# A fused attention and SwiGLU kernel: one hand-paced order replaced by a build-time planner, with batch 0 in two halves

## Chip, cores and metric

The kernel runs on one core of a Trainium2 chip. The metric is the device time of one execution in microseconds (us); times of several executions are given as a median.

The core's engines work side by side, each through its own queue in order: PE (matrix products, with PEld its weight loads), DVE (elementwise), ACT (functions and copies), POOL (here mostly the issue of loads) and SP (the issue of transposing DMAs and of output stores). They wait for each other by semaphores. Products land in PSUM, eight banks of 512 fp32 columns on 128 partitions; ACT and DVE must empty a bank before it is used again.

## The reference

Attention with squared ReLU in place of softmax, for 8 batches and 12 heads, 448 tokens, head size 64; then an RMS norm and a gated FFN on the 3584 tokens by 768 features.

```python
def _attn_ref(q, k, v):
    scale = 1.0 / np.sqrt(q.shape[-1])
    scores = scale * np.matmul(q, k.transpose(0, 1, 3, 2))
    attn = np.maximum(scores, 0.0) ** 2 / S
    return np.matmul(attn, v)

def _moe_ref(x, w_gate, w_val, w_out, rms_g):
    rms = np.sqrt(np.mean(x * x, axis=-1, keepdims=True) + 1e-06)
    xn = x / rms * rms_g
    g = xn @ w_gate
    silu = g * (1.0 / (1.0 + np.exp(-g)))
    val = xn @ w_val
    return silu * val @ w_out
```

Inputs and output are fp32 in memory; the kernel loads them as bf16 and accumulates in fp32. The hidden width is 1536.

## The kernel before

**Products by halves of the array.** The head size is 64, so PE's array is used as two row halves of 64 rows: two products, one on each half, run at the same time. A pair of them is called a step here. The class `Stream` (L306) pairs the two halves of the FFN's products: a `Group` (L357) is one output tile; first its lower half runs as the leading one of the pair while the group before it runs its upper half, then it follows. `emit` (L375) writes one half product and, when a group changes halves, a wait on PE for its own last product.

**Attention of one batch** (`attention`, L281) goes over six pairs of heads `j`. For batches 0 and 1 q and k are turned by PE (`transposes`, L169, copied by DVE, L182); later ones by transposing DMAs on SP (`transpose_dma`, L100). `scores` (L208) computes 128 keys by 448 queries for two heads into a pair of PSUM banks (psS), three times per `j`; the last 64 keys of two `j` share one tile (`rest_scores`, L221). `rectify` (L197) empties each: relu to bf16 on ACT (L202) or DVE (L200) by the fixed table `relu_on`, then a square in place on DVE (L205), for three tiles of batch 0 on POOL. `attend` (L238) multiplies by v for two `j` as 64-by-64 products on the four quarters of the array (psAV); ACT scales into xT (L276) and DVE squares xT into x2 (L278).

**Norm.** `norm_sums` (L402; `norm`, L408, for batch 0) multiplies the six tiles of x2 by a matrix of ones: six steps into psSS. `norm_scale` (L418) takes the square root on ACT (L420), loads the SiLU table, takes the reciprocal on DVE (L424) and scales xT to xn in six instructions (L427).

**FFN.** `ffn` (L503): 12 gate and 12 value groups of six steps of 448 columns (psP), emptied by `silu` on ACT (L451) and by `hidden` on DVE (L456) into hT. Then output tiles of 128 tokens, in three pieces of 256 columns (`OW`, L474), 12 steps each (psO): three tiles after an even batch, four after an odd one, as two batches share 7 tiles. `store` (L486) copies on ACT (L490) and, after the third piece, issues the output from SP (L498).

**Order.** Loads of batch 0, the gate and value weights in eight slices, then batch 0's attention and norm run alone; `keep_busy` (L137) writes products of zeros on PE into psB, 16 at the start, one after each `scores` and 24 during the norm. Loads of batch 1 and w_out stand in POOL's order after that. From then the loop at L523 lays the attention of batch b+1 as `side` units between the FFN steps of batch b, evenly by a cost that counts columns. The sum for the norm goes to the front of the stream after the last attend.

PSUM: two pairs of banks for scores and attends (`ps_s`) and four single banks for all else (`ps_m`).

Of the kernel before, what the change touches and what calls it, by code (L numbers as in the profile page):

```python
# [9 lines left out]
I32 = mybir.dt.int32  # L10
# [4 lines left out]
NCH = 4  # L15
U = 7
UH = 4


@with_exitstack  # L20
def kernel(
# [22 lines left out]
    NT = 2 * S // P  # L44

# [6 lines left out]
    apool = ctx.enter_context(tc.tile_pool(name="attn", bufs=12))  # L52
    xpool = ctx.enter_context(tc.tile_pool(name="xT", bufs=1))
    npool = ctx.enter_context(tc.tile_pool(name="norm", bufs=2))
    hpool = ctx.enter_context(tc.tile_pool(name="hT", bufs=2))
    spool = ctx.enter_context(tc.tile_pool(name="sig", bufs=3))
    opool = ctx.enter_context(tc.tile_pool(name="ostage", bufs=3))
    ps_s = ctx.enter_context(tc.tile_pool(name="ps_s", bufs=2, space=bass.MemoryType.PSUM))
    ps_m = ctx.enter_context(tc.tile_pool(name="ps_m", bufs=4, space=bass.MemoryType.PSUM))

    ld = {}
    qkT = {}
    src_of = {"q": q, "k": k, "v": v}
    PE_T = 2

    def load(nm, b, h0=0, h1=H):
# [7 lines left out]
        t = ld[nm, b]  # L76
        src = src_of[nm][b, h0:h1]
        if nm == "q":
            parts = [(slice(0, PC), PC, 0, NCH)]
        else:  # L80
            parts = [(slice(0, D), D, 0, UH), (slice(D, P), D, UH if nm == "k" else UH - 1, U)]
        for prt, n, u0, u1 in parts:
            if runs:
                nc.gpsimd.dma_start(  # L84
                    out=t[prt, h0:h1, : (u1 - u0) * D],
                    in_=src.rearrange("h (p u) d -> p h (u d)", p=n)[:, :, u0 * D : u1 * D],
                )
            else:
                to = t[prt].rearrange("p u (h d) -> p u h d", d=D)
                rows = src.rearrange("h (p u) d -> p u h d", p=n)  # L90
                step = u1 - u0 if nm == "q" else 1
                for u in range(u0, u1, step):
                    nc.gpsimd.dma_start(  # L93
                        out=to[:, u - u0 : u - u0 + step, h0:h1, :], in_=rows[:, u : u + step]
                    )

    def new_qkT(b):
        qkT[b] = qtpool.tile([P, HP, 2, S], BF16, name="qkT", tag="qkT")

    def transpose_dma(b):  # L100
        new_qkT(b)
        for c in range(UH):
            n = P if c < UH - 1 else D
            nc.sync.dma_start_transpose(
                out=qkT[b][:, :, 0, c * P : c * P + n], in_=ld["k", b][:n, c, :]
            )
        for c in range(NCH):
            nc.sync.dma_start_transpose(
                out=qkT[b][:, :, 1, c * PC : (c + 1) * PC], in_=ld["q", b][:, c, :]
            )  # L110
# [5 lines left out]
    FS = F // NSL  # L116

    def load_w(which, s):
        dst, src = {"g": (wg_sb, moe_w_gate), "v": (wv_sb, moe_w_val)}[which]
        nc.gpsimd.dma_start(  # L120
            out=dst[:, :, s * FS : (s + 1) * FS],
            in_=src.rearrange("(kt p) f -> p kt f", p=P)[:, :, s * FS : (s + 1) * FS],
        )

    def load_wo(s, n):
        w = FT // n
        nc.gpsimd.dma_start(
            out=wo_sb[:, s * w : (s + 1) * w, :],
            in_=moe_w_out.rearrange("(fk p) m -> p fk m", p=P)[:, s * w : (s + 1) * w, :],
        )  # L130
# [5 lines left out]

    def keep_busy(n):  # L137
        ps = ps_m.tile([P, S], FP32, name="psB", tag="mm")
        for _ in range(n):
            nc.tensor.matmul(out=ps[:], lhsT=ones_bf[:], rhs=busy_bf[:], start=True, stop=True)  # L140

    load("q", 0, 0, 2)
    load("k", 0, 0, 2)
    ident = const.tile([P, P], BF16, name="ident", tag="ident")
    masks.make_identity(nc, ident[:])
# [3 lines left out]

    def act_table(func):  # L150
        nc.scalar.activation(out=scrap[:], in_=eps_col[:], func=func)

    act_table(ACT.Sqrt)
    g_sb = wpool.tile([P, KT], FP32, name="g_sb", tag="rmsg")
    nc.sync.dma_start(out=g_sb[:], in_=moe_rms_g.rearrange("(kt p) -> p kt", p=P))
    load("q", 0, 2, 6)
    load("k", 0, 2, 6)
    load("v", 0, 0, 6)
    load("q", 0, 6, 12)
    load("k", 0, 6, 12)  # L160
    load("v", 0, 6, 12)
    for s in range(NSL):
        load_w("g", s)
        load_w("v", s)

    behind = mybir.DependencyInfo(mybir.DependencyClass.Sync, mybir.DependencyReason.DATA)
    xTs = {}

    def transposes(b, j):  # L169
        if j == 0:  # L170
            new_qkT(b)
        psT = ps_m.tile([P, 2, S], BF16, name="psT", tag="mm")
        flat = psT[:].rearrange("p t s -> p (t s)")
        for nm, n, w, at in (("k", P, UH, 0), ("q", PC, NCH, S)):
            for c in range(w):
                for hh in range(2):
                    nc.tensor.transpose(  # L177
                        out=flat[hh * D : (hh + 1) * D, at + c * n : at + (c + 1) * n],
                        in_=ld[nm, b][:, 2 * j + hh, c * D : (c + 1) * D],
                        identity=ident[:n, :n],  # L180
                    )
        nc.vector.tensor_copy(out=qkT[b][:, j, :, :], in_=psT[:])  # L182

    rsq = {}
    pending = []

    def relu_on(b, j, c):
        return "dve" if c == UH - 1 or (b and j % 2 and c == 2) else "act"

    def square_on(b, j, c):  # L190
        return "pool" if b == 0 and j >= 3 and c == 1 else "dve"

    def flush():
        while pending:
            pending.pop(0)()

    def rectify(b, j, c, psS):  # L197
        r = apool.tile([P, 2, S], BF16, name="r", tag="r")
        if relu_on(b, j, c) == "dve":
            nc.vector.tensor_relu(out=r[:], in_=psS[:, :, :S])  # L200
        else:
            nc.scalar.activation(out=r[:], in_=psS[:, :, :S], func=ACT.Relu)  # L202
        eng = nc.gpsimd if square_on(b, j, c) == "pool" else nc.vector
        flush()
        pending.append(lambda: eng.tensor_tensor(out=r[:], in0=r[:], in1=r[:], op=ALU.mult))  # L205
        rsq[b, j, c] = r

    def scores(b, j, c):  # L208
        psS = ps_s.tile([P, 2, 512], FP32, name="psS", tag="psS")
        for hh in range(2):  # L210
            prt = slice(hh * D, (hh + 1) * D)
            nc.tensor.matmul(  # L212
                out=psS[:, hh, :S],
                lhsT=qkT[b][prt, j, 0, c * P : (c + 1) * P],
                rhs=qkT[b][prt, j, 1, :],
                start=True,
                stop=True,
            )
        rectify(b, j, c, psS)

    def rest_scores(b, j):  # L221

        psS = ps_s.tile([P, 2, 512], FP32, name="psS", tag="psS")
        for hh in range(2):
            prt = slice(hh * D, (hh + 1) * D)
            for jj in range(2):
                nc.tensor.matmul(  # L227
                    out=psS[jj * D : (jj + 1) * D, hh, :S],
                    lhsT=qkT[b][prt, j + jj, 0, (UH - 1) * P : (UH - 1) * P + D],
                    rhs=qkT[b][prt, j + jj, 1, :],  # L230
                    start=True,
                    stop=True,
                )
        return psS

    x2s = {}

    def attend(b, j, then=None):  # L238
        psAV = ps_s.tile([P, 2, 512], FP32, name="psAV", tag="psS")
        v = ld["v", b]  # L240
        rest = rsq[b, j, UH - 1]
        low, high = slice(0, D), slice(D, P)
        pairs = {
            low: [[(rsq[b, j + jj, i], i) for i in range(UH - 1)] for jj in range(2)],
            high: [[(rsq[b, j + jj, i], i + 1) for i in range(UH - 1)] for jj in range(2)],
        }
        pairs[low][0].append((rest, UH - 1))
        pairs[high][1].append((rest, 0))
        last = {}

        def run(first):
            for step in range(UH - (not first)):
                for prt, jj in ((low, 0), (high, 1)) if first else ((low, 1), (high, 0)):
                    r, u = pairs[prt][jj][step]
                    for hh in range(2):
                        if not first and step == 0:
                            tc.add_manual_dep(nc.tensor.nop().ins, last[jj, hh].name, behind)
                        mm = nc.tensor.matmul(  # L258
                            out=psAV[hh * D : (hh + 1) * D, jj, :S],
                            lhsT=v[prt, 2 * (j + jj) + hh, u * D : (u + 1) * D],  # L260
                            rhs=r[prt, hh, :],
                            start=(first and step == 0),
                            stop=(not first and step == UH - 2),
                        )
                        last[jj, hh] = mm.ins

        run(True)
        psR = rest_scores(*then) if then else None
        run(False)
        if j == 0:  # L270
            xTs[b] = xpool.tile([P, KT, S], BF16, name="xT", tag="xT")
            x2s[b] = npool.tile([P, KT, S], BF16, name="x2", tag="x2", bufs=1)
        xT = xTs[b][:, j : j + 2, :]
        if then:
            rectify(*then, UH - 1, psR)
        nc.scalar.mul(out=xT, in_=psAV[:, :, :S], mul=inv_attn)  # L276
        pending.append(
# [302 lines left out]
```

## Time and profile before

| | |
|---|---|
| runs | 467.36, 470.43, 467.46 us; median 467.46 |
| span of the profiled execution, first to last instruction | 466.5 us (its own time is not listed apart) |
| mean granted clock of PE | 0.982 of full |
| HBM read, written | 48.76 MB, 11.01 MB |
| last matmul starts | 461.2 us |

The costliest groups, by line (us busy and mean ns of one):

| group | count | busy | mean |
|---|---|---|---|
| L380 psP, gate and value products | 2268 recorded | 456.8 | 349 |
| L380 psO, 256 columns | 2016 | 139.6 | 271 |
| L202 relu on ACT, 128x896 from PSUM | 123 | 111.1 | 918 |
| L205 square on DVE, 128x896 bf16 | 165 | 100.9 | 628 |
| L456 hidden on DVE, 128x448 | 96 | 59.5 | 620 |
| L451 silu on ACT, 128x448 | 96 | 51.9 | 542 |
| L200 relu on DVE, 128x896 from PSUM | 45 | 49.1 | 1090 |
| L490 output copy on ACT, 128x256 | 84 | 30.5 | 372 |
| L427 xn on DVE, 128x448 | 48 | 29.3 | 680 |
| L424 reciprocal on DVE, 128x448 | 8 | 23.6 | 2953 |
| L276 xT on ACT, 128x896 | 24 | 22.0 | 917 |
| L140 psB, products of zeros | 58 | 17.6 | 418 |

A product's duration includes its way through the array, and two to four run at once, so the busy time of single products is no cost; the distance between starts is. Some matmul records are missing (2268 of 2304 psP products are there). Start times in the views are in us from the first instruction; "<-" names what a group writes and reads.

### The profile page before, as it was taken

The numbers are of one execution on the slowest core, as the hardware profiler recorded it, in microseconds if no ns is written. First come the engines' busy times: TensorE is split into PE (matmuls) and PEld (weight loads), VectorE is DVE, ScalarE is ACT, GpSimd is POOL, SyncE is SP. The second block draws the span as 40 slices with busy tenths as digits, with TensorE's granted clock in tenths as the row PEclk, the third lists the DMA queues.
The fourth block names the chain that finished last, engine by engine and source line by source line (L and its number), as shares of the span: only waits on it lengthen the run. The fifth ranks groups of instructions, "written<-read, shape, count | busy, mean of one in ns | idle before, by whom it ended". The sixth has DMA issues, their size and how long they took to land.

```text
span 466.5 us, 12798 instructions
## 1 busy us (share of the span) xinstructions
PE 453.6 (97%) x5722; PEld 292.8 (63%) x5722; DVE 274.0 (59%) x403; ACT 234.9 (50%) x360; POOL 80.6 (17%) x97
## 2 busy tenths in 40 slices
PE   6989999999999999999999999999999999999995
PEld 3434655676666766676666766676667766676674
DVE  1676378866663867576566657576656677332200
ACT  1682246665645655375445755465535764532221
POOL 8438211571007000340007000100000000000000
PEclk8698999999999999999999999999999999999998
DMA  9999999799907970299209960438002200020013
GB/s 106 194 204 199 206 173 162 80 204 165 127 3 107 214 124 2 23 200 146 44 1 124 211 109 1 58 82 135 20 1 54 85 2 1 2 84 20 1 42 95
DMA packets 130758, 44.47 MB, mean 95 GB/s; under 512 B 102928, under 2 KB 127120, under 8 KB 130704
## 3 DMA queue, kind: packets, MB, share of 16 engines
q0 software_dynamic: 91648, 24.39, 54.1%
q1 hardware_dynamic: 39056, 19.28, 20.5%
q8 instruction: 44, 0.72, 0.6%
q14 instruction: 10, 0.08, 0.0%
HBM read 48.76 MB, written 11.01 MB: 128 GB/s over the span
## 4 chain that ended last, share of the span: by engine, by line
PE 91%; DVE 3%; ACT 2%; DMA 1%; POOL 1%; issue 1%; POOLq 0%
PE psP L380 47%; PE psO L380 23%; PE psAV L258 8%; PE psS L212 6%; PE psSS L380 2%; ACT r L202 2%; PE psB L140 1%; PE psT L177 1%; PE psS L227 1%; DMA kb<-in_k_dram 1%; DVE xn L427 1%; PE psP L441 1%; DVE r L200 1%; DVE r L205 1%; DVE rstd L424 1%
## 5 line engine op out<-in xcount | busy, mean ns | idle before, releaser
L380 PE MATMUL psP<-xn,wv_sb 64*128 64x448 bf16 x1140 | 229.0, 349 | 0.0
L380 PE MATMUL psP<-xn,wg_sb 64*128 64x448 bf16 x1128 | 227.8, 349 | 0.1
L380 PE MATMUL psO<-wo_sb,hT 64*128 64x256 bf16 x2016 | 139.6, 271 | 0.0
L202 ACT ACTIVATE r<-psS 128x896 bf16<-128x896 f32 x123 | 111.1, 918 | 47.5 <-PE psS L212 46.8
L380 PEld LDWEIGHTS <-wv_sb 64*128 64x128 bf16 x1140 | 96.1, 94 | 41.5 <-issue 4.3
L380 PEld LDWEIGHTS <-hT 64*128 64x128 bf16 x2016 | 101.1, 94 | 33.0 <-issue 2.9
L380 PEld LDWEIGHTS <-wg_sb 64*128 64x128 bf16 x1128 | 94.3, 94 | 35.6 <-issue 1.3
L205 DVE TENSOR_TENSOR r<-r 128x896 bf16<-128x896 bf16 x165 | 100.9, 628 | 16.3 <-ACT r L202 15.6
L456 DVE TENSOR_TENSOR hT<-sil,psP 128x448 bf16<-128x448 bf16 x96 | 59.5, 620 | 79.7 <-PE psP L380 52.4
L451 ACT ACTIVATE sil<-psP 128x448 bf16<-128x448 f32 x96 | 51.9, 542 | 74.7 <-PE psP L380 68.8
L200 DVE TENSOR_SCALAR r<-psS 128x896 bf16<-128x896 f32 x45 | 49.1, 1090 | 31.7 <-PE psS L227 24.2
L212 PE MATMUL psS<-qkT 64*128 64x448 bf16 x288 | 59.3, 358 | 1.9 <-DVE r L200 1.2
L490 ACT COPY ost<-psO 128x256 f32<-128x256 f32 x84 | 30.5, 372 | 43.5 <-PE psO L380 39.6
L276 ACT ACTIVATE xT<-psAV 128x896 bf16<-128x896 f32 x24 | 22.0, 917 | 54.4 <-PE psAV L258 50.1
L258 PE MATMUL psAV<-r,vb 64*64 64x448 bf16 x672 | 43.9, 361 | 1.8 <-POOL r L205 1.2
L84 POOL DMA_DIRECT2D vb<-in_v_dram x18 | 13.2, 750 | 167.7 <-PE psO L380 122.3
L424 DVE RECIPROCAL rstd<-rstd 128x448 f32<-128x448 f32 x8 | 23.6, 2953 | 26.0 <-ACT rstd L420 26.0
L93 POOL DMA_DIRECT2D kb<-in_k_dram x42 | 33.0, 1008 | 18.7 <-DMA wo_sb<-in_moe_w_out_dram 9.6
L258 PEld LDWEIGHTS <-vb 64*64 64x64 bf16 x672 | 17.3, 106 | 22.3 <-issue 10.3
L427 DVE SCALAR_TENSOR_TENSOR xn<-xT,g_sb,rstd 128x448 bf16<-128x448 bf16 x48 | 29.3, 680 | 0.3
L212 PEld LDWEIGHTS <-qkT 64*128 64x128 bf16 x288 | 19.8, 94 | 11.4 <-issue 6.2
L140 PE MATMUL psB<-busy_bf,ones_bf 128*128 128x448 bf16 x58 | 17.6, 418 | 1.3 <-DVE busy_bf L135 1.3
(38 smaller groups left out, 161.7 us busy)
## 6 DMA issues: line engine op xcount, KB each, us to landing
vb<-in_v_dram POOLq DMA_DIRECT2D x14, 384.0 KB, 7.2
qb<-in_q_dram POOLq DMA_DIRECT2D x7, 672.0 KB, 12.9
kb<-in_k_dram POOLq DMA_DIRECT2D x43, 96.0 KB, 12.7
out_dram<-ost SPq DMA_DIRECT2D x8, 336.0 KB, 4.1
wg_sb<-in_moe_w_gate_dram POOLq DMA_DIRECT2D x4, 576.0 KB, 16.5
wv_sb<-in_moe_w_val_dram POOLq DMA_DIRECT2D x4, 576.0 KB, 18.1
wo_sb<-in_moe_w_out_dram POOLq DMA_DIRECT2D x2, 1152.0 KB, 21.4
out_dram<-ost SPq DMA_DIRECT2D x8, 288.0 KB, 4.4
```

Of the source, the lines that this page charges most:

```text
L93: nc.gpsimd.dma_start(out=to[:, u - u0 : u - u0 + step, h0:h1, :], in_=rows[:, u : u + step])
L200: nc.vector.tensor_relu(out=r[:], in_=psS[:, :, :S])
L202: nc.scalar.activation(out=r[:], in_=psS[:, :, :S], func=ACT.Relu)
L205: pending.append(lambda: eng.tensor_tensor(out=r[:], in0=r[:], in1=r[:], op=ALU.mult))
L212: nc.tensor.matmul(out=psS[:, hh, :S], lhsT=qkT[b][prt, j, 0, c * P : (c + 1) * P], rhs=qkT[b][prt, j, 1, :], start=True, stop=True,)
L258: mm = nc.tensor.matmul(out=psAV[hh * D : (hh + 1) * D, jj, :S], lhsT=v[prt, 2 * (j + jj) + hh, u * D : (u + 1) * D], rhs=r[prt, hh, :], s ...
L380: mm = nc.tensor.matmul(out=self.ps[:, : self.w], lhsT=self.lhsT(i)[prt], rhs=self.rhs(i)[prt], start=(half == 0 and i == 0), stop=(half = ...
L424: nc.vector.reciprocal(out=rstd[:], in_=rstd[:])
L427: nc.vector.scalar_tensor_tensor(out=xn[:, kt, :], in0=xTs[b][:, kt, :], scalar=g_sb[:, kt : kt + 1], in1=rstd[:], op0=ALU.mult, op1=ALU.mult,
L451: nc.scalar.activation(out=s[:], in_=psG[:], func=ACT.Silu)
L456: nc.vector.tensor_tensor(out=hTs[b // 2][:, fb, o : o + S], in0=sil[b, fb][:], in1=psV[:], op=ALU.mult)
L490: nc.scalar.copy(out=ost[:, o : o + w], in_=ps[:, :w])
```

## The change

The whole order is now made when the kernel is built, by a `Planner`: each instruction group is an `Op` with assumed durations on the engines it may run on, what it depends on, a rank, and the PSUM banks and ring buffers it needs. The planner walks a simulated time: at each point it takes the engine that can start something first, and there the ready operation of lowest rank. Relu and output copies go to ACT or DVE, whichever the plan has free first. The operations are written out in that order.

- Batch 0 is attended in two halves of 224 queries (`halves`, `HS`), each with its own norm and its own 24 gate and value groups of 224 columns; from batch 1 on the width is 448.
- The norm: ACT takes a logarithm and then exp(-0.5 x), both in one table set (`LN_EXP`), in place of root and reciprocal. DVE adds the squares of the three pairs in fp32 (`square`, `close`), so the sum over features is one product with ones, except in batch 0's first half.
- Output pieces are 384 columns wide, two to a tile (`OW`); copies go to ACT or DVE.
- Groups of 448 columns are emitted as four 64-by-64 quarter products per step (`quarters`), scores beside them too.
- xT, xn and rstd have two buffers; squares never run on POOL; hT has one buffer in place of two; 14 relu buffers in place of 12.
- All loads of batches 0 and 1 and the weights are issued at the start, v of batch 0 after q and k; products of zeros (`fill`) stand where the plan finds PE idle.

```diff
+    def choose(self, e):
+        cands = self.candidates(e)
+        step = None
+        if e == "PE" and self.stream is not None:
+            step = self.stream.earliest()
...
+        for r, rank, n, op, s in cands:
+            if r <= t + 1e-9:
+                if op.due is not None:
+                    rank = -1 if op.due() else 1
+                key = (rank, n)
+                if best is None or key < best[0]:
+                    best = (key, op, s)
...
+    pairs = [psum.tile([P, 2, 512], FP32, name=f"psS{i}", tag=f"psS{i}") for i in range(4)]
+    wide = [Space(pairs[i], (2 * i, 2 * i + 1)) for i in range(4)]
+    single = [Space(pairs[i // 2][:, i % 2, :], (i,)) for i in range(4, 8)]
...
+    def blocks():
+        return ((0, D), (D, P)) if state["quarters"] else ((0, P),)
...
+        rl = add(Op({"ACT": 0.14 + n * 0.833e-3, "DVE": 0.13 + n * 1.042e-3}, relu,
+                    [t] + r_ring.before, rank=2, lean={"DVE": 0.9}))
+        on = {"DVE": 0.06 + n * 0.53e-3}
+        sq = add(Op(on, square, [rl], rank=3))
...
+        def square(op):
+            x = xTs[b][:, j : j + 2, lo : lo + w]
+            acc = accs[b, lo][0][:, :, :w]
+            dst = x2[:, :, :w] if j else acc
+            nc.vector.tensor_tensor(out=dst, in0=x, in1=x, op=ALU.mult)
+            if j:
+                nc.vector.tensor_tensor(out=acc, in0=acc, in1=dst, op=ALU.add)
+
+        def close(op):
+            acc, total, _ = accs[b, lo]
+            nc.vector.tensor_tensor(
+                out=total[:, :w], in0=acc[:, 0, :w], in1=acc[:, 1, :w], op=ALU.add
+            )
...
+            act_set(LN_EXP)
+            nc.scalar.activation(
+                out=rstd[:, :w], in_=g.ps[:, :w], func=ACT.Ln, scale=1.0 / float(DM),
+                bias=eps_col[:],
+            )
+            nc.scalar.activation(out=rstd[:, :w], in_=rstd[:, :w], func=ACT.Exp, scale=-0.5)
...
+            state["quarters"] = any(g.quarters for _, g in pair)
+            for m in blocks():
+                for half, g in pair:
+                    g.emit(half, *m)
...
+        op = add(Op({"ACT": lambda: 0.14 + w * 0.833e-3 + switch(SILU)}, fn, [g.end], rank=0,
+                    ring=sil_ring))
...
-    OW = DM // 3
+    OW = DM // 2
...
+    attention_half(0)
+    stream.add([norm_sums(0, 0, HS)])
     for b in range(B):
+        groups = ffn(b)
         if b == 0:
+            stream.add(groups[:24])
+            plan.run(lambda: (0, 0) in summed)
+            attention_half(HS)
+            attention_full(1)
+            stream.add(groups[24:])
+            sums = [norm_sums(0, HS, HS), norm_sums(1, 0, S)]
```

## The prediction

> **What bounds the kernel now.** I read the engine totals first, then the chain of waits in order of time, then the PE timeline inside one stage, then the DMA issues. The totals, first list of the page (busy us, share, instructions):
>
> ```profile
> PE 453.6 (97%) x5722; PEld 292.8 (63%) x5722; DVE 274.0 (59%) x403; ACT 234.9 (50%) x360; POOL 80.6 (17%) x97
> ```
>
> PE is almost always busy, DVE and ACT little over half. The ends of matmuls are modelled, so 97% does not say that all of it is needed; the chain does (start us, us, what). The opening:
>
> ```profile
> 5.15 4.30 DMA kb<-in_k_dram
> ...
> 34.87 1.40 DVE r L205
> 36.27 0.04 issue
> 36.31 2.27 PE psAV L258 x18
> ...
> 40.81 4.65 PE psB L140 x24
> 45.45 3.53 PE psP L441 x36
> ```
>
> Until 45.4 no FFN product runs: batch 0's attention goes from engine to engine, and psB, which computes nothing, covers its norm. Then the chain is PE nearly to the end, with one more hole before batch 1's FFN:
>
> ```profile
> 95.49 0.64 ACT rstd L420
> 96.13 0.02 issue
> 96.15 2.96 DVE rstd L424
> 99.12 0.02 issue
> 99.14 3.68 DVE xn L427 x6
> ```
>
> PE works through that on output pieces; batch 1's FFN really starts at 102.4. Later stretches are pure PE, here around batch 4:
>
> ```profile
> 289.31 1.32 PE psP L380 x14
> ...
> 297.77 0.11 PE psO L380
> 297.88 0.08 PE psP L380
> ...
> 308.92 0.90 PE psO L380 x16
> ```
>
> Fourteen half products are seven steps (both row halves at once), so a 448-column step is 0.189 us; sixteen psO are eight steps of 256 columns, 0.1125 each. Where both widths meet, the chain alternates: the narrow half idles. The PE timeline at an attend (start, us, then the group):
>
> ```profile
> 179.64 0.35 PE L380 MATMUL psP<-xn,wv_sb 64*128 64x448 bf16 x1
> 179.92 0.95 PE L258 MATMUL psAV<-r,vb 64*64 64x448 bf16 x16
> 180.93 0.79 PE L258 MATMUL psAV<-r,vb 64*64 64x448 bf16 x12
> 181.66 0.36 PE L380 MATMUL psP<-xn,wg_sb 64*128 64x448 bf16 x1
> ```
>
> From the psP step at 179.64 to the next at 181.66 lie 2.02 us. Eight quarter steps (32 instructions with four rest scores) and one psP step make 9 x 0.189 = 1.70; about 0.3 goes at the changes of shape and the in-order wait inside. I take 0.2 an attend as theirs.
>
> **Part by part.** The sum is made against the span, 466.5; the median of the runs is 467.46, 1.0 above. The profiled execution's own time is not listed apart, so I put 1.0 around the span.
>
> *Steady part, 102.4 to PE's end at 461.2.* It holds six batches' attentions, seven projections and 25 output tiles.
>
> - Sum for the norm: six psSS steps become one, since DVE adds the squares first. 5 x 0.189 x 6 batches = 5.7. Twelve steps that pair 448 with 256 columns go as well: the narrow half loses 0.189 - 0.1125 = 0.077 in each, half of the array: 12 x 0.077 / 2 x 6 = 2.8.
> - Pieces of 384: interpolating the two step rows (0.0004 us per column) gives 0.164, an estimate. A tile costs 24 x 0.164 = 3.93 for 36 x 0.1125 = 4.05; 25 tiles save 3.0. Bounds: nothing gained, or 5. The meeting of widths is cheaper, 0.189 - 0.164 = 0.025 for 0.077: 12 steps a batch x 0.052 / 2 x 7 = 2.2.
> - Quarter products: projections of full width and scores are emitted as four 64-by-64 products, the shape of attends, so the change of shape goes: 18 attends x 0.2 = 3.6. PE's instructions in these steps double. The attend shows four loads and four products per 0.189 us step (16 in 0.88, chain), so I cost the doubling at nothing, though its longest run is 32 products.
>
> Sum 17.3.
>
> *Engines beside it.* Between 263.2 and 368.5 (two batches, 105.3 us) DVE is busy 68.4 and ACT 59.0. A batch loses the reciprocal (2.95) and three bf16 squares (0.62 each) and gets five fp32 squares or adds of 896 plus a half one. No fp32 tensor product is in the trace; the nearest rows bound it by 0.63 (L205, bf16) and 1.09 (L200, fp32 read from PSUM). I take 1.0, as it reads or writes fp32: 5.5 - 4.8 = +0.7 us a batch, hidden under 18 us of idle DVE; uncovered it would cost 0.7 x 7 = 5. ACT gains one more pass of 0.63 a batch, with one table set for log and power, so still two loads of 1.28. Both have cover. Two-tile norm buffers let the next norm run ahead.
>
> The Trainium skill, "VectorE: DVE Perf Modes", section "The perf-mode tier table", puts fp32 tensor_tensor at the slowest rate; an estimate from its formula, (896+151)/0.96 ns, is 1.09 us, at my upper row, and would make the batch +1.2.
>
> *Batches 0 and 1.* Transfers do not get shorter. The weight slices land in a row, the last of eight 24.0 us after its issue at 18.1:
>
> ```profile
> wv_sb<-in_moe_w_val_dram POOLq DMA_DIRECT2D x1, 576.0 KB, 24.0
> ```
>
> That is 42.1; the first value slice landed at 24.3 (11.3 + 13.0), so a slice takes 3.0 us. Half of batch 0: evictions and squares are half of before, the last q and k land at 15.7 (8.45 + 7.2); chain by rows: last scores, 0.9 eviction, 0.6 square, products, 0.5 out, squares, two passes, xn, about 9 us: FFN from about 25 in place of 45.4. But it is paced by slices to 42, and batch 1's q and k (1344 KB at 192 KB/us) end at 49, so the twenty us do not all count. What counts is when batch 1's FFN can start. From 47 its attention needs, by rows: 21 evictions (20 us), 21 squares (13), copies (3.7), xT (2.8), squares for the norm (5.6), with batch 0's second-half silu and products (8.4) and output copies (2.9): 56 us over ACT and DVE, 28 each, 31 at 90% use, then norm 4. That is 82; with 4 for unevenness, **86**, instead of 102.4: 16.4 gained. PE has 54 us of products for 25 to 86, so it is not the limit here, even if the 224-column steps of batch 0 (0.100 by the same interpolation, against a 94 ns load that must fit) take 0.11: 288 x 0.01 = 3 us, inside the 7 spare. Fill products stand only where the plan sees PE idle. Bounds: 80 if nothing waits, 98 if late transfers (w_out, 61.9 before) hold the output pieces.
>
> Loads of batch 1 come in ten issues for five on POOL, which now holds no squares (1.70 each on POOL, now 0.63 on DVE); nothing but loads is queued there. On SP, transposes and output stores share the queue as before.
>
> *What the plan costs.* Each engine's order is fixed from assumed durations: square 0.535 (row 0.628), relu on ACT 0.886 (0.918), silu 0.513 (0.542). Per batch 21 x 0.093 + 21 x 0.032 + 12 x 0.03 = 3.0 us too little. In-order PE waits where a product was put just behind an eviction, with the whole FFN stream queued after it. If all lateness reached PE: 7 x 3 = 21. As idle time of a third on both engines takes most, I take 4.
>
> Sum: 466.5 - 17.3 - 16.4 + 4 = 436.8, time **438**. Own range 428 to 449 (batch 1's start 80 to 96, plan 0 to 10). The tail from PE's end, 5.3 us, stays.
>
> **Rivals.**
>
> 1. *The plan drifts* (0.13): the 21 us reach PE instead of 4: 455. For it: only two pairs of PSUM banks for scores and attends, so PE waits at once when a relu is late. Against: the present order, paced without any model, lets PE run unbroken.
> 2. *The head gives nothing* (0.06): batch 1's FFN starts at 98, as transfers and ACT/DVE set it: 450.
> 3. *Quarters are issue-bound*, the slower case (0.08). The densest long row is psO: four instructions per 0.1092 to 0.1125 us, 27 to 28 ns each. If 27.3 were the floor, eight take 0.218, not 0.189: 7 x 144 projections and about 200 others, 1,210 steps x 0.029 = 35: 473. It decides above 0.217 a step. Against: the attend's 23.6 ns an instruction, and psO fits its columns without a floor.
> 4. *Gains cancel* (0.04): half of each of these, 463 to 472.
>
> The Trainium skill, "TensorEngine Tiling (Array Packing)", section "Tiling Modes", says that a change of mode drains the array, which agrees in sign with the 0.3 above; its section "Restrictions and Gotchas" speaks against the change: column tiling gives up fast weight load. The row shows 105 ns for a 64*64 load and 94 for 64*128. If the two loads of a row half came one after the other, 210 ns would exceed 189 and 1,210 steps would cost 25 us, giving 463; the attend's rows speak against that.
>
> **How the numbers follow.** Forecast 0.69, rivals 0.13, 0.06, 0.08, 0.04. The range 426 to 457 takes in the forecast and the first two and leaves out rivals 3 and 4 and a little below. About 1% is what can be told from no change. Faster by over 1% (below 462.8): 0.87; within: 0.05; slower: 0.08.
>
> **What would show it.** Right: first psP of batch 0 near 25, of batch 1 near 86; step 0.189 in quarters and 0.16 in pieces; one sum step; no gap at attends. Wrong: quarter steps over 0.2; PE waiting on relu, square or xn in every batch; DVE over 80% busy; PE waiting on w_out.

## The result, and the profile after

The changed kernel takes 597.04 us (median, 595.80 to 597.47), against 467.63 us of the kernel before in the same session: a ratio of 1.276, 95% interval 1.272 to 1.280. The forecast was 438, with a range of 426 to 457. The profiled execution has a span of 594.9 us, 128 more than before.

The totals of the kernel after, first list of its page (busy us, share of the span, instructions):

```profile
PE 493.9 (83%) x7789; PEld 311.9 (52%) x7789; DVE 250.4 (42%) x411; ACT 273.0 (46%) x388; POOL 78.5 (13%) x99
```

DVE has less to do than before and ACT 38 us more, both under half of the span. No engine became the bound; PE's share fell from 97% to 83%. The chain that ended last, by engine and by line:

```profile
PE 76%; DVE 10%; ACT 10%; issue 3%; DVEq 0%; ACTq 0%
PE psS L738 61%; DVE hT L802 8%; PE psS L537 7%; ACT sil L788 5%; PE psS L424 4%; ACT ost L859 2%; PE psS L965 2%; PE psS L368 1%; ACT r L406 1%; DVE x L574 1%; ACT xT L564 1%; PE psS L460 1%; PE psS L442 1%; DVE acc L576 0%; DVE qkT L378 0%
```

Before, PE had nearly all of it:

```profile
PE 91%; DVE 3%; ACT 2%; DMA 1%; POOL 1%; issue 1%; POOLq 0%
```

Now 23% of the chain, 137 us, is not PE, and most of that lies on the three lines that empty the FFN's banks: hT, sil and ost, 15% of the span together. The waits say who waits for them (engine and line, waited for: us in all, times, longest us):

```profile
PE psS L738 <- DVE hT L802: 51.0, 76, 0.8
...
PE psS L738 <- ACT sil L788: 21.6, 40, 0.6
...
PE psS L738 <- ACT ost L859: 10.8, 20, 0.6
```

PE waited for none of these before. One place shows the form of it: the last batch's FFN, where no attention runs beside it. The timeline of the kernel after (start us, us, what; in brackets the idle time before and what ended it):

```profile
530.17 0.54 ACT L788 ACTIVATE sil<-psS 128x448 bf16<-128x448 f32 x1 [3.53 <-PE psS L738]
530.77 0.35 PE L738 MATMUL psS<-xn,wg_sb 64*64 64x448 bf16 x1 [0.63 <-ACT sil L788]
...
532.20 0.62 DVE L802 TENSOR_TENSOR hT<-sil,psS 128x448 bf16<-128x448 bf16 x1 [3.45 <-PE psS L738]
...
532.88 0.35 PE L738 MATMUL psS<-xn,wv_sb 64*64 64x448 bf16 x1 [0.78 <-DVE hT L802]
```

ACT had been idle for 3.53 us and DVE for 3.45, so neither is late. PE finishes a group, stands while that group's bank is read, and only then begins the next one, although four banks are there and two groups are in work at a time. A group takes 2.0 to 2.1 us; six steps of 0.189 are 1.13. The windows view of the whole stretch (us, then busy us of PE, PEld, DVE, ACT, POOL; clock, DMA share, GB/s):

```profile
515.80:568.40 52.60, 35.24 (x633) 21.95 (x633) 6.84 (x11) 7.49 (x14) 0.00 (x0) 1.00 0.06 17
```

### The profile page after: what moved, and what is told of

It is laid out like the page before. It is cut to its first block, busy times and chain, and to the rows that moved or that the text cites. A ratio compares the mean times of both kernels' runs of the same rounds, so it can differ in the third digit from the quotient of the medians.

```text
span 594.9 us, 16977 instructions
## 1 busy us (share of the span) xinstructions
PE 493.9 (83%) x7789; PEld 311.9 (52%) x7789; DVE 250.4 (42%) x411; ACT 273.0 (46%) x388; POOL 78.5 (13%) x99
## 4 chain that ended last, share of the span: by engine, by line
PE 76%; DVE 10%; ACT 10%; issue 3%; DVEq 0%; ACTq 0%
PE psS L738 61%; DVE hT L802 8%; PE psS L537 7%; ACT sil L788 5%; PE psS L424 4%; ACT ost L859 2%; PE psS L965 2%; PE psS L368 1%; ACT r L406 1%; DVE x L574 1%; ACT xT L564 1%; PE psS L460 1%; PE psS L442 1%; DVE acc L576 0%; DVE qkT L378 0%
## 5 line engine op out<-in xcount | busy, mean ns | idle before, releaser
L738 PE MATMUL psS<-xn,wv_sb 64*64 64x448 bf16 (+1 forms) x2304 | 226.4, 341 | 52.5 <-DVE hT L802 39.6
L738 PE MATMUL psS<-xn,wg_sb 64*64 64x448 bf16 (+1 forms) x2304 | 232.3, 341 | 18.4 <-DVE hT L802 9.5
L406 ACT ACTIVATE r<-psS 128x896 bf16<-128x896 f32 (+1 forms) x164 | 143.5, 907 | 89.4 <-PE psS L424 74.0
L738 PEld LDWEIGHTS <-wg_sb 64*64 64x64 bf16 (+1 forms) x2304 | 121.0, 105 | 102.2 <-issue 80.6
L738 PE MATMUL psS<-wo_sb,hT 64*128 64x384 bf16 (+1 forms) x1514 | 157.0, 324 | 17.1 <-ACT ost L859 9.7
L738 PEld LDWEIGHTS <-wv_sb 64*64 64x64 bf16 (+1 forms) x2304 | 120.1, 105 | 68.8 <-issue 50.0
L410 DVE TENSOR_TENSOR r<-r 128x896 bf16<-128x896 bf16 (+1 forms) x171 | 101.7, 613 | 82.7 <-ACT r L406 82.2
L738 PEld LDWEIGHTS <-hT 64*128 64x128 bf16 (+1 forms) x1514 | 87.3, 96 | 63.1 <-issue 33.7
L802 DVE TENSOR_TENSOR hT<-sil,psS 128x448 bf16<-128x448 bf16 (+1 forms) x108 | 61.4, 569 | 127.3 <-PE psS L738 119.5
L788 ACT ACTIVATE sil<-psS 128x448 bf16<-128x448 f32 (+1 forms) x108 | 54.2, 503 | 89.5 <-PE psS L738 85.3
```

The lines of the kernel that those rows point to most:

```text
L406: nc.scalar.activation(out=op.view, in_=src, func=ACT.Relu)
L410: eng.tensor_tensor(out=rl.view, in0=rl.view, in1=rl.view, op=ALU.mult)
L738: mm = nc.tensor.matmul(out=self.ps[m0:m1, : self.w], lhsT=self.lhsT(i)[prt, m0:m1], rhs=self.rhs(i)[prt], start=(half == 0 and i == 0), s ...
L788: nc.scalar.activation(out=s[:, :w], in_=g.ps[:, :w], func=ACT.Silu)
L802: nc.vector.tensor_tensor(out=hT[:, fb, o : o + w], in0=sil[b, fb, lo][1][:, :w], in1=g.ps[:, :w], op=ALU.mult,)
```

## The experiments

### Which edit costs 129 us: the single banks as halves of a tile

The kernel before has four single banks, each a tile of its own (`ps_m`). The diff makes them halves of two tiles, `pairs[i // 2][:, i % 2, :]`. **Theory:** waits are set for a tile, so a product into one half waits until the neighbour half has been read. **Rivals:** quarters are limited by the number of instructions; or the planner's short durations make PE late.

Banks apart need batch 0's first half to do without the two further pairs, so `e0_two_pairs` does that alone, and `e1_own_tiles` gives each bank its tile on top of it. `q0_no_quarters` is the changed kernel without quarters. `b1_before_shared` is the kernel before with its four banks as halves of two tiles, taken from a free list; `b0_before_list` has the same list and four tiles.

```diff
 e0:
-  pair=wide if b == 0 and lo == 0 else wide[:2]
+  pair=wide[:2]
 e1, on top of e0:
-  pairs = [psum.tile([P, 2, 512], ...) for i in range(4)]
-  single = [Space(pairs[i // 2][:, i % 2, :], (i,)) for i in range(4, 8)]
+  pairs = [psum.tile([P, 2, 512], ...) for i in range(2)]
+  ones = [psum.tile([P, 512], FP32, ...) for i in range(4)]
+  single = [Space(ones[i - 4][:, :], (i,)) for i in range(4, 8)]
 q0:
-  state["quarters"] = any(g.quarters for _, g in pair)
+  state["quarters"] = False
 b1 (b0 keeps four tiles [P, 512]):
+  two = [ps_m.tile([P, 2, 512], FP32, ...) for i in range(2)]
-  self.ps = ps_m.tile([P, 512], FP32, name=self.name, tag="mm")
+  self.ps = bank(id(self))       # two[n // 2][:, n % 2, :]
```

> The changed kernel, batch 0's first half confined to the two score pairs of PSUM (it used all four), all else as it is; a control for the next run. Theory (the four single banks are halves of two tiles, and a product into one half waits for the reading of the other half): 585 to 610 us, as 597 now. Rival A (quarter products are limited by issue): the same. Rival B (the plan's durations are too short, so PE waits in order): the same.

> As the control, but each of the four single banks is a tile of its own; the planner sees the same banks. Theory of the shared tiles: the waits of first products for silu, hidden and output copies go, 425 to 450 us. Rival A: over 560, the quarter steps stay slow. Rival B: over 560, PE still waits for late engines.

> The changed kernel with full 64x128 products instead of quarters everywhere in the stream, tiles as they are. Theory of the shared tiles: 580 to 610 us, no gain. Rival A: 440 to 480. Rival B: 580 to 610.

> The kernel before with its four single banks made halves of two tiles, taken from a list in the order in which they come free; nothing else of the change. Theory of the shared tiles: 520 to 620 us, slower by the wait of each of some 290 groups for its neighbour's reading, 0.2 to 0.5 us each. Rivals A and B: 465 to 475, no difference.

> The kernel before with its four single banks taken from the same free list as in the run where they were halves of two tiles (627.6 us), but each a tile of its own. If the shared tile is what cost 160 us there, this one is at 465 to 475, as the kernel before; if the free list's order of banks had a part in it, it is well over 480.

| kernel | us | against before |
|---|---|---|
| e0: tiles shared, two pairs | 630.92 | one run |
| **e1: a tile for each bank** | **461.07** | 0.984 (0.980 to 0.988) |
| q0: after, no quarters | 582.86 | one run |
| b1: before, banks shared | 627.55 | one run |
| b0: before, same list, own tiles | 467.73 | one run |

e0 and e1 differ in nothing but the tiles, and lie 170 us apart. So do b1 and b0: 160 us, in a kernel with no planner and no quarters. Without quarters the changed kernel is still at 583. The waits of b1:

```profile
PE two L394 <- DVE hT L471: 47.8, 61, 1.8
...
PE two L394 <- ACT sil L466: 35.4, 55, 1.3
...
PE two L394 <- ACT ost L507: 26.0, 51, 1.2
```

They are the same three as after the change. In e1 none of them is left; its totals and chain:

```profile
PE 448.0 (97%) x7829; PEld 338.1 (74%) x7829; DVE 243.4 (53%) x405; ACT 268.7 (58%) x394; POOL 78.5 (17%) x99
...
PE 96%; ACT 1%; issue 1%; DVE 0%; ACTq 0%
```

Its last FFN, the same products that took 53 us above, takes 30:

```profile
407.70:438.00 30.30, 30.30 (x632) 28.77 (x633) 6.83 (x11) 7.49 (x14) 0.00 (x0) 1.00 0.10 29
```

The theory stands; both rivals fall as causes of the loss. Three expectations missed in size: e1 gains less than I expected, and e0 and b1 lose more. e0's edit touches only batch 0, yet it costs 34 us more than the changed kernel. In the traces batch 1's FFN begins 3.8 us later (117.9 for 114.1), so 30 of the 34 come after it, where only the plan's order can differ. What a shared tile costs therefore seems to depend on which groups the plan puts side by side in it; no run shows that. What is left to explain is e1's 461 against a forecast of 438.

### The parts one at a time, with the banks apart

Each run undoes one part in e1, which has all of them; `p1_longer_durations` changes the planner's figures alone.

```diff
 q1:
-  state["quarters"] = any(g.quarters for _, g in pair)
+  state["quarters"] = False
 o1:
-  OW = DM // 2
+  OW = DM // 3
 p1 (the others alike, by 0.02 to 0.09):
-  on = {"DVE": 0.06 + n * 0.53e-3}
+  on = {"DVE": 0.15 + n * 0.53e-3}
 h1:
-  return ((0, HS), (HS, HS)) if b == 0 else ((0, S),)
+  return ((0, S),)
-  attention_half(0)
-  stream.add([norm_sums(0, 0, HS)])
+  attention_full(0)
+  stream.add([norm_sums(0, 0, S)])
```

> The kernel with a tile for each of the four single banks (461.1 us), and no product in quarters: one instruction of 128 columns where there were two of 64. Theory 1, the tail of the saving lies in the attends: the quarters win 18 attends x 0.2 = 3.6 us there, so without them 464 to 466. Theory 2, the quarters' doubled instructions and their turns of the array's mode at the P-to-O transitions (about 1.35 us a transition with them, 0.9 to 1.1 in the kernel before) and their extra instruction fetches in batch 1 and 2's stage take more than that back: without them 453 to 459. If the two cancel, 460 to 463.

> The same kernel with the output projection in three pieces of 256 columns in place of two of 384. By the prediction's term the 384-column pieces save 3.0 us in the products and 2.2 in evictions, so 464 to 467 without them. If the longer pieces only move the wait to the evictions of 384 columns (two pieces to a bank pair instead of three), 459 to 462.

> The same kernel with the planner's durations for relu, square, silu, the attend's eviction, the fp32 square and the output copy raised by 0.02 to 0.09 us to the rows measured in the profile. The prediction charged the too-short durations 4 us: if they cost that, 456 to 458. If the order hardly depends on them, 460 to 462; if longer durations make the planner leave gaps, 463 to 468.

> The same kernel with batch 0 whole, as batches 1 to 5 are, in place of two query halves. The prediction gave the early start of the first FFN 16.4 us of gain. If that gain reaches the end, 472 to 480 here. If what the head wins is given back while batch 1 runs (its FFN ends 6 us earlier than before, though it starts 12 earlier), because batch 2's q and k land no sooner, 463 to 470. If nothing of it reaches the end, 459 to 462.

Measured: q1 **455.74** (0.974, 0.972 to 0.976), o1 471.85 (1.007, 1.004 to 1.010), p1 462.23 (0.987, 0.984 to 0.991), h1 464.62 (0.992, 0.989 to 0.995).

**Quarters cost 5.3 us**, as theory 2 expected; of its causes some show below, and one is only argued. Of the 5.3 us, 3.3 fall in one stage: batch 2's FFN begins at 156.3 in e1 and 152.9 in q1, batch 1's at 95.0 and 94.9. The windows of batch 1's gate and value products, e1 and then q1:

```profile
95.00:132.70 37.70, 34.92 (x693) 22.82 (x689) 22.12 (x35) 23.04 (x33) 10.19 (x12) 1.00 1.81 132
```

```profile
95.00:130.00 35.00, 34.81 (x393) 18.44 (x390) 22.27 (x35) 23.05 (x33) 10.40 (x12) 1.00 1.54 137
```

This is about the same work with 300 more products; PE's busy time is nearly equal, and PE is idle for 2.8 us where it was idle for 0.2. The timeline of e1 shows the longest hole:

```profile
121.39 0.36 PE L739 MATMUL psM<-xn,wg_sb 64*64 64x448 bf16 x4
123.06 0.37 PE L739 MATMUL psM<-xn,wg_sb 64*64 64x448 bf16 x1 [1.32 <-issue]
```

PE waits for nothing that the profile can name ("issue"). e1 has three holes of this kind in the stage, q1 none. The kernel has 17,067 instructions instead of 12,331, and the DMA engines are about nine tenths busy here; that PE waits for its own instructions is possible, but only argued. The other 2 us are small losses at later stages, such as these where value products end and output pieces go on alone in e1:

```profile
238.57 0.35 PE L739 MATMUL psM<-xn,wv_sb 64*64 64x448 bf16 x2
238.86 0.82 PE L739 MATMUL psM<-wo_sb,hT 64*128 64x384 bf16 x8
239.61 0.37 PE L739 MATMUL psM<-ssum,ones_bf 64*64 64x448 bf16 x1
```

The last quarter products start at 238.57. One step later, 0.19, the next could start; it starts after 0.29, 0.10 late. Eight half products of 384 columns take 0.65 at their steady pace, and the next start is 0.75 later: again 0.10. Quarters remove such turns at the attends and make them here.

**384 columns** are worth 10.8 us, twice the prediction's 5.2 and more than either outcome that I had expected. **Short durations** cost nothing that can be measured. **Two halves** are worth 3.5 us, not 16.4: with batch 0 whole the first FFN product starts at 40.9 instead of 29.5, but batch 1's FFN at 98.9 instead of 95.0, and from there both kernels take the same time.

### Pairs of parts, the sum for the norm, and the attends

Three runs start from q1. `qo_256_no_quarters` has pieces of 256 columns. `qs_six_sums` squares in bf16 and has six ones-products for each norm, as before. `qa_covered_attends` puts up to two FFN steps, in quarters, between the halves of each attend.

```diff
 qs:
-  sq = add(Op({"DVE": cost}, square, [ev], rank=2))
+  sq = add(Op({"DVE": 0.06 + 2 * w * 0.53e-3}, square_bf, [ev], ...))
-  1, w, lambda i: ones_bf[:], lambda i: accs[b, lo][1][:, :w],
+  KT, w, lambda i: ones_bf[:], lambda i: x2_of[b % 2][:, i, lo : lo + w],
 qa:
   for first in (True, False):
+      if not first:
+          for _ in range(2):
...
+              took = stream.step(at)
```

> The kernel without quarters (455.7 us) and with output pieces of 256 columns. With quarters the 256-column pieces cost 10.7 us (471.9 against 461.1), twice the 5.2 of the prediction. If quarters and short pieces make it worse together (more pieces beside quartered products, so more turns between 64- and 128-column products), about 5 us here: 459 to 462. If the pieces alone are worth it all, 465 to 468.

> The kernel without quarters, with the squares in bf16 and six ones-products for each norm, as the kernel before has them, in place of the fp32 sum on VectorE and one ones-product. The prediction gives the one product 5 x 0.189 x 6 = 5.7 us: 460 to 463 here if that is so. If the sum on VectorE puts back what it saves, because the norm's Ln waits longer for it at each transition, 454 to 458.

> The kernel without quarters, with up to two steps of the feed-forward products (these in quarters, so that the array need not change) between the two halves of each attend, where the rest products stood in the kernel before and where the trace now shows starts 0.41 us apart in place of 0.19. If each of these waits costs 0.2 us, the 18 attends give 3 to 4 us: 451 to 453. If the waits only move, 455 to 457; if the added turns of the array cost more, 458 to 462.

Measured: qo 465.42 (0.995, 0.993 to 0.997), qs 463.60 (0.991, 0.987 to 0.994), qa 453.60 (0.971, 0.966 to 0.975). The pieces are worth 9.7 without quarters, so they need no help from them: the second of the two outcomes expected. The sum by DVE with one ones-product is worth 7.9, a little more than expected. Covering the attends gains 2.1, less than the 3 to 4 expected; the intervals of q1 and qa overlap.

Taken one by one, the parts come to 7.9 + 9.7 + 3.5 - 5.3 = 15.8, while e1 has gained 6.6. The last four runs ask where 9 us go. `n0_planner_only` has none of the four parts (qs, o1, h1 and q1 in one); `n0a_planner_covered` adds qa's edit to it; `qh_whole_no_quarters` is q1 with h1's edit; `qb_covered_from_batch2` is qa with the cover from batch 2 on:

```diff
-                if not first:
+                if not first and b >= 2:
```

> The planner's order and the norm by log and power alone: own tiles for the single banks, no quarters, batch 0 whole, six ones-products, output pieces of 256 columns. If the parts add up, the order itself costs some 9 us over the kernel before: 455.7 + 9.7 + 7.9 + 3.5 = 477, so 472 to 480. If the parts overlap (each is worth more beside the others than alone) and the order costs nothing, 465 to 469.

> The same with up to two steps of products between the halves of each attend, in the place where the rest products stood before. If the attends' inner waits are most of what the order costs, 4 us or more under n0_planner_only; if the cost is elsewhere (which attends stand between feed-forward and output products, the mixed widths there), 0 to 3 us under it.

> The kernel without quarters (455.7 us), with batch 0 whole. With quarters the halves were worth 3.5 us. In the trace the 576 half-array products of 224 columns start 52.3 ns apart in place of 46.1 for each half of a 448-column one, which is 3.6 us given back of an FFN that starts 11 us earlier. If the value of the halves has nothing to do with quarters, 458 to 461; if the quarters were what ate it, 463 to 468.

> The kernel without quarters, with products between the halves of the attends from batch 2 on alone. With them in all attends (453.6 us) the stretch from batch 1's FFN on was 2.7 us shorter than without (350.7 against 353.4), but batch 1's FFN began 3.4 us later (98.3 against 94.9). Keeping the first without the second gives 450 to 452.5; if the start moves all the same, 453 to 456.

Measured: n0 472.36 (1.010, 1.007 to 1.012), n0a 464.92 (0.993, 0.991 to 0.996), qh 459.28 (0.981, 0.979 to 0.984), **qb 453.34** (0.968, 0.965 to 0.971). The rest is split: the order with the new norm and buffers costs 4.8 over the kernel before, and the parts overlap by 4.5 (from n0 to q1 is 16.6, not 21.1). Covering the attends gives n0 7.4 us, 0.31 for each of 24, more than all the order costs there. The halves are worth 3.5 with and without quarters. qb has the lowest median, but qa's 453.60 is not to be told from it; both beat the kernel before and the changed one. qb missed the 450 to 452.5 that it was made for: batch 1's FFN began at 96.4 in it, against 94.9 in q1 and 98.3 in qa, so the start moved although nothing was put into the attends before batch 2.

PE's timeline at an attend in q1, where nothing stands between its halves:

```profile
318.48 1.81 PE L538 MATMUL psS<-r,vb 64*64 64x448 bf16 x28
320.09 0.39 PE L461 MATMUL psS<-qkT 64*64 64x448 bf16 x4
320.41 0.55 PE L739 MATMUL psM<-xn,wg_sb 64*128 64x448 bf16 x4
```

and in qb:

```profile
317.80 0.95 PE L550 MATMUL psS<-r,vb 64*64 64x448 bf16 x16
318.58 0.55 PE L751 MATMUL psM<-xn,wg_sb 64*64 64x448 bf16 x8
318.96 0.74 PE L550 MATMUL psS<-r,vb 64*64 64x448 bf16 x12
319.53 0.36 PE L461 MATMUL psS<-qkT 64*64 64x448 bf16 x4
319.82 0.55 PE L751 MATMUL psM<-xn,wg_sb 64*128 64x448 bf16 x3
```

and in e1, where the FFN products around it are quarters too:

```profile
322.90 1.81 PE L538 MATMUL psS<-r,vb 64*64 64x448 bf16 x28
324.51 0.39 PE L461 MATMUL psS<-qkT 64*64 64x448 bf16 x4
324.70 0.76 PE L739 MATMUL psM<-xn,wg_sb 64*64 64x448 bf16 x10
```

q1 takes 1.93 us (318.48 to 320.41) for eight quarter steps, 1.51 at 0.189: 0.42 lost. qb takes 2.02 for ten, 1.89: 0.13 lost, though two FFN steps were added. e1 takes 1.80 for the same eight as q1: 0.29 lost. The kernel before had its rest products between the halves and took 1.74 for eight (179.92 to 181.66): 0.23 lost.

## Why the prediction was wrong

**The step that failed** is the one that took PSUM as before. The prediction reads "only two pairs of PSUM banks for scores and attends" and goes on to count work; it takes the four single banks for as free of each other as they were, though the diff it had in front of it makes them halves of two tiles. That is no size of a term but a wait that was left out, in the one resource that every FFN group passes through. It costs 136 us (597.0 against 461.1, where e1 also takes the two further pairs from batch 0's first half; 160 and 170 in the two pairs of runs that differ in the tiles alone). The prediction named "PE waiting" as the sign of being wrong, but for relu, square and xn; it came from sil, hT and ost.

With the banks apart the forecast is still 23 us short. By the prediction's own marks, in the profiled execution of e1, 9.0 of it lie before batch 1's FFN, which starts at 95.0 and not at 86: 7.4 us gained of 16.4. From there to PE's last start it takes 359.1 us, where 358.8 - 17.3 + 4 = 345.5 were expected: 13.6 more. By the runs that change one part each, the same 23 us split otherwise:

- **Batches 0 and 1: 12.9.** 16.4 predicted; the two halves are worth 3.5. The rest of the 7.4 is not theirs: with batch 0 whole, batch 1's FFN still starts at 98.9 (h1) and 100.1 (n0), and what that brings is counted below. Two parts of the working failed. The first FFN product came at 29.5, not 25. And PE hardly had a pause after it, where the prediction saw "54 us of products for 25 to 86". In q1 the products from 30.1 to 94.9 come to about 54 us, counted by columns at the pace of full steps, and take 64.8, with no two starts more than 0.51 us apart; the chain leaves PE there once, for 5 us of ACT's work from 46.45 on. The 224-column steps are not the reason: in the middle of a group one takes 0.096, even less than the 0.100 interpolated. (The 52.3 ns in an expectation above is a mean that takes in half products without a partner.) The 10 us go in small pieces, at half products without a partner and at the turns between transposes, scores, attends and FFN products; no run separates them. Transfers landing late, the reason for the upper bound, did not decide.
- **Quarters: 8.9.** -3.6 predicted, +5.3 measured. Rival 3's floor fell: quarter products start 47.2 ns apart, so a step is 0.189, as at the attend. The 0.2 at an attend was right for the same order: counted by columns, from about 1 us before an attend to 1 us after it, 0.56 us are lost in q1 and 0.37 in e1 (medians). But the kernel before loses 0.37 there as well. The plan had moved the rest products out from between an attend's halves, so the wait inside, which the prediction left as it was, grew by as much as the quarters gave. What failed beside that is the doubling of the instructions, costed at nothing: outside the attends quarters lose about 9 us (5.3 + 18 x 0.19), in the holes of batch 1's stage and at turns such as those to the output pieces.
- **Sum and pieces: 0.6,** and that is luck. 8.5 and 5.2 predicted, 13.7; from n0 to q1, less the halves, 13.1. Singly the sum is 7.9 and the pieces 9.7, but they overlap. And the pieces do not gain where the prediction had it. One whole output tile in the chains of q1 (384 columns) and qo (256):

```profile
242.22 3.90 PE psM L739 x48
...
247.66 3.93 PE psM L739 x72
```

So 25 tiles save 0.8 us in products, not 3.0. The prediction's 4.05 came from 0.1125 a step; this row gives 0.109. The gain lies where the widths meet, which the prediction put at 2.2 in all. In each of batches 2 to 6, 27 half products of 384 columns stand between the first and the last FFN product in q1, and 22 of 256 in qo: 4736 columns more, about 1.0 us at 0.2125 ns a column. The stretch of output pieces between two batches' FFN products is 1.3 to 1.5 us shorter in q1, six times over; the rest of that was not followed.
- **The plan: 0.8,** again partly luck. 4 charged for short durations, 4.8 measured for the order, but not for that reason: p1 shows no gain from longer ones, and rival 1, that the plan drifts, fell with it. In the profiled execution n0 begins batch 1's FFN 2.3 us earlier than the kernel before and takes 5.5 more from there; n0a, with the attends covered, gets 7.4 back.
- **DVE and ACT** stayed hidden, as argued. The fp32 squares and adds took the upper row. The groups of e1, by form (us busy, mean ns of one):

```profile
L577 DVE TENSOR_TENSOR acc<-acc,x 128x896 f32<-128x896 f32 x14 | 15.3, 1092 | 0.5
```

Here the Trainium skill ("VectorE: DVE Perf Modes", section "The perf-mode tier table"), which puts fp32 tensor_tensor at the slowest rate, was right where I went below it: the estimate from the page's formula was 1.09, I took 1.0. On quarters, its "TensorEngine Tiling (Array Packing)", section "Restrictions and Gotchas", says that column tiling excludes fast weight load; my estimate of 25 us for that did not come, as the 0.189 us step shows. The section "Tiling Modes" of the same page says that a change of mode drains the array; the 0.10 us lost at such turns in e1 agrees with it.

12.9 + 8.9 + 0.6 + 0.8 = 23.2, the distance from 438 to 461.1. They must add up, as the runs form a chain (before, n0, q1, e1); that each stands for its part rests on the runs that changed one thing.

## What to carry to other kernels

When a diff moves buffers, ask first which tile each view belongs to, and who reads the other views of it: two banks in one tile gave the waits of one bank. An engine idle before it empties a bank, and PE idle until it has, is the sign; giving each bank its own tile is the cheapest run to try. And value an early start only by the start of the next stage that has no slack: 11.4 us at the first product were 3.9 one batch later.

## What the runs showed of the hardware

- In the middle of a group, half products start 94.5 ns apart at 448 columns, 81.3 at 384, 54.6 at 256 and 48 at 224: 0.211, 0.212, 0.213 and 0.214 ns a column. Down to 224 columns a narrow product costs hardly more for each column. What costs is a half product without a partner: the last ones of q1, of 384 columns, start 163 ns apart.
- Four quarter products keep the pace of two half products (47.2 ns an instruction against 94.5), but with them PE stood idle for up to 1.32 us at a time in the stage with busy DMA engines, put down to "issue". Why was not settled: no run changed the number of instructions alone.
- Products with 64 and with 128 columns of the array in turn lost about 0.1 us at each change (238.57 and 238.86 in e1).
